# A Fourier stage whose first batch has a buffer of its own, filled in seven parts during the attention

## The chip, the cores and the metric

The kernel runs on one core of a Trainium2 chip. The metric is the device time of one execution in microseconds (us). The time before is the median of three runs.

## The reference

An attention, a Fourier mixing block with an MLP, and a gated block follow one another. `B`=4 batches, `H`=8 heads, `S`=576 positions, head size 64, width 512.

```python
scores = q @ k^T / sqrt(64) + bias
x = softmax(scores) @ v                       # (4, 576, 512)
mixed = real(fft(fft(x, axis=1), axis=2))
u = x + mixed
un = (u - mean(u)) / sqrt(var(u) + 1e-6)
y = u + relu(un @ w_ch1) @ w_ch2              # 512 -> 2048 -> 512
h = relu(y @ w_in); a, v = halves(h)
out = (a * (w_spatial @ norm(v) + b_spatial)) @ w_out
```

## The kernel before

The kernel makes the bias (to about 142 us), runs the attention, then the Fourier stage, then the MLP and the gated block. Only the attention's last two thirds and the Fourier stage are touched here.

**Attention** (`attention_phase`). It goes in 72 double steps `d` (two halves of a head's queries) through a software pipeline: scores on PE (line 408), row maximum on DVE (421), exponential `P` on ScalarE (444), one or more steps later. `P` has to be transposed for the product with `v`. For the even steps below 68 ScalarE (455) and POOL (461) cast `P` to an f16 tile `hl`, each a part of it, and a DMA transpose on SP's queue (474) makes `pt`; for the odd ones and the last four PE transposes `P` itself (484) and ScalarE (486) and DVE (493) evict it. PE multiplies (510), DVE normalises (539, 548) into `x`, and SP stores `x` into DRAM, one tensor `xd[b]` for a batch (560, 563). POOL also prepares the next head's operands (385, 387, 390, 393), ScalarE casts them (382, 383, 392). At the end of step `d` a hook `after(n)` is called with n = d - 72; it is `first_folds`.

**Fourier stage** (`Folds`, `fft_phase`). Real input makes it enough to work on sums and differences of a row and its mirror. `Folds.load(b)` reads `xd[b]` into a tile of six chunks of 128 rows: chunks 0 to 2 plain (rows 0 to 255, and 33 rows from 256; SP, lines 734, 735), chunks 3 to 5 the rows in reversed order, gathered by row number from POOL (line 737; 127, 128 and 32 rows), with single rows set to zero (732, 733). `Folds.steps` makes with DVE sums `T0` and differences `T1` of the two halves (748), the same along the width (`X0`, `X1`, 760), and the folds `F00` to `F11` (765). The names in the rows are `lowb` and `dif` for `T0` and `T1`, `uv`, `F`. On PE `stage1` makes four products for a batch, `pe`, `me`, `po`, `mo` (line 860), into one of two PSUM banks `y`, which ScalarE evicts (864). `corner(b)` copies one column of the tile to another (867, `raw<-raw 128x6`), `gather` makes `near` (871), which PE transposes into `xs` (878); `second` makes `D` (888), evicted as `d` (895), and DVE adds both (898, 906). Batch 0's load is made at n=-5, at the end of the attention, batch 1's at n=2, batch 2's at n=5, and some of batch 0's folds at n=3, 4, 5; batch 3's load is in the plan. Batch 0's tile is `raw`; those of batches 1 to 3 and the sums `T0` lie in `lowb`.

**What sets the order.** In the attention the order is the program's. In the Fourier stage a planner (`Plan.run`) sorts all operations, those of the first MLP weights (`w0` to `w3`) and of the layer norm among them: it takes each time the operation whose start, by given durations, less a bonus from the table `RANK` is least; `READY` gives the time from which a batch's tile counts as there. Each engine then works in its order, apart from what the compilation may move ahead where an operation depends on nothing between. A tile of MLP weights is loaded by SP (1676, `w<-in_w_ch`), squared on ScalarE (1015, `wsq<-w`) and split with DVE's help (1022 to 1028, 1684). The first MLP matmul is line 1339.

```python
    if d == nd:
        e1.close()
    after(d - nd)
```

Of the kernel before, what the change touches and what calls it, by code (L numbers as in the profile page):

```python
# [9 lines left out]
F32 = mybir.dt.float32  # L10
# [8 lines left out]
B, H, S, D = 4, 8, 576, 64  # L19
# [41 lines left out]
def pool(tc, **kw):  # L61

    return tc.tile_pool(reuse_waits="tile", **kw)
# [281 lines left out]
def attention_phase(tc, nc, io, vs, bias, biasl, raw, xd, ident, after, es, right):  # L345
# [206 lines left out]
    def store(d):  # L552
# [8 lines left out]
        for a in range(2):  # L561
            f = 128 * p + (64 * a if ahead(n) else 64 - 64 * a)
            nc.sync.dma_start(out=xd[b][512:S, f : f + 64], in_=x[64 * a : 64 * a + 64, 4, 0:64])

    yield [lambda n=n, nm=nm: load(n, nm) for n in range(2) for nm in "kqv"]
    yield from prep(0)
    yield True
# [13 lines left out]
    for d in range(nd + L5 + 2):  # L581
# [43 lines left out]
        if us and n + 2 < len(pairs):  # L625
            for nm in {0: "k", 1: "q", 2: "v"}.get(c - 5 * (c >= 5), ""):
                load(n + 2, nm)
# [7 lines left out]
def phases(tc, nc, io, vs, low, raw, xd, ident, tables, after, right):  # L635

    n = 2 * H * S
    bias = [x[:, 0:n].rearrange("p (t h s) -> p t h s", t=2, h=H) for x in low]
    biasl = low[1][:, n : n + NP * S].rearrange("p (h s) -> p h s", h=NP)
    with ExitStack() as es:  # L640
        att = attention_phase(tc, nc, io, vs, bias, biasl, raw, xd, ident, after, es, right)
        ready = False
        loads = next(att)

        def early(n):
            nonlocal ready
            if n >= Q_LOAD and loads:
                loads.pop(0)()
            if n >= T_LOAD:
                next(tables, None)  # L650
            if n in Q_PREP:
                ready = ready or next(att)

        with ExitStack() as e:
            bias_phase(tc, nc, io, vs, bias, biasl, early, e)
        while not ready:
            ready = next(att)
        for _ in att:
            pass
# [4 lines left out]
W_SCALE = 2.0**-112  # L664
TP = 290
T2 = 289
F_LOAD = -5
X_LOAD = 2, 5
FOLDS = {3: 3, 4: 3, 5: 2}
YB = 2  # L670
AFTER = (0,)
PRINT = False
RANK = {
# [4 lines left out]
}  # L678
READY = 0.0, 3.0, 8.0, 14.0


def tables(tc, nc, io, es):

    cp = es.enter_context(pool(tc, name="dft", bufs=1, side="right"))


    tt = cp.tile([128, 2, 3, TP], F32, name="tt")

    fs = cp.tile([128, 7, 128], F32, name="fs")
    ident = cp.tile([128, 128], F32, name="ident")  # L690
    rows = cp.tile([128, 3], I32, name="rows")

    def load():
        nc.gpsimd.dma_start(out=tt, in_=io["c_t"])
        yield
        for k in (slice(0, 4), slice(4, 7)):
            nc.sync.dma_start(out=fs[:, k], in_=io["c_f"][:, k])
            yield
        nc.sync.dma_start(out=ident, in_=io["c_ident"])
        nc.sync.dma_start(out=rows, in_=io["c_rows"])  # L700
        yield

    return (tt, fs, ident, rows), load()


class Folds:
# [19 lines left out]
        for F in self.two:  # L726
            self.nc.gpsimd.memset(F[1][:, :, 0:1], 0.0)

    def load(self, b):
        nc, x, d = self.nc, self.xs[b], self.xd[b]  # L730
        f = slice(1, DM + 1)
        nc.gpsimd.memset(x[32:33, 5, f], 0.0)
        nc.gpsimd.memset(x[0:1, 3, f], 0.0)
        nc.sync.dma_start(out=x[:, 0:2, f], in_=d[0:256].rearrange("(k p) d -> p k d", p=128))
        nc.sync.dma_start(out=x[0:33, 2, f], in_=d[256:T2])
        for k, r in ((3, slice(1, 128)), (4, slice(0, 128)), (5, slice(0, 32))):
            nc.gpsimd.indirect_dma_start(
                x[r, k, f], None, d[:, :],
                bass.IndirectOffsetOnAxis(ap=self.rows[0 : r.stop - r.start, k - 3 : k - 2], axis=0),
            )  # L740

    def steps(self, b):

        nc, x, F = self.nc, self.xs[b], self.two[b % 2]
        op = ALU.add, ALU.subtract

        def total(z):
            nc.vector.tensor_tensor(
                out=self.sums[z][:, :, 1 : DM + 1], in0=x[:, 0:3, 1 : DM + 1], in1=x[:, 3:6, 1 : DM + 1], op=op[z]
            )  # L750

        def mix(z):
            w = self.sums[z]

            def two(start, step):
                return bass.AP(
                    tensor=w.tensor, offset=w.offset + start, ap=[list(w.ap[0]), [DM + 2, 3], [step, 2], [-1, 129]]
                )

            nc.vector.tensor_tensor(out=self.uv[z], in0=two(256, 129), in1=two(513, -385), op=op[z])  # L760

        def fold(z, y):
            u, v = self.uv[z][:, :, 0], self.uv[z][:, :, 1, ::-1]
            o, r = (((0, slice(0, 129)), (129, slice(0, 128))), ((1, slice(1, 128)), (128, slice(1, 129))))[z][y]
            nc.vector.tensor_tensor(
                out=F[z][:, :, o : o + r.stop - r.start], in0=u[:, :, r], in1=v[:, :, r], op=op[y]
            )

        for z in range(2):
            yield f"T{z}", 1.75, lambda z=z: total(z)  # L770
            yield f"X{z}", 0.96, lambda z=z: mix(z)
            for y in range(2):
                yield f"F{z}{y}", 0.55, lambda z=z, y=y: fold(z, y)


def first_folds(folds):

    todo = []

    def after(n):  # L780
        if n == F_LOAD:
            folds.load(0)
        if n == 0:
            folds.open()
            todo.extend(folds.steps(0))
        if n in X_LOAD:
            folds.load(1 + X_LOAD.index(n))
        for _ in range(FOLDS.get(n, 0)):
            todo.pop(0)[2]()

    return after
# [45 lines left out]
def fft_phase(tc, nc, folds, tabs, ut, bank, extra, es):  # L837
# [28 lines left out]
    def corner(b):  # L866
        nc.scalar.activation(out=xs[b][:, :, 0:1], in_=xs[b][:, :, 256:257], func=AF.Copy)
# [45 lines left out]
    for b in range(B):  # L913
# [3 lines left out]
        if b:  # L917
            last = (b - 1, "F11") if b > 1 else None
            for nm, us, go in folds.steps(b):
                add_op(  # L920
                    (b, nm), f"fold{b}", [("DVE", us)], go, after=([last] if last else []) + (["load"] if b == B - 1 else []),
                    take=[f] if nm == "F00" else [], start=READY[b],
                )
                last = b, nm
        for nm, us, need in (("pe", 1.5, "F00"), ("me", 1.5, "F01"), ("po", 3.0, "F10"), ("mo", 1.5, "F11")):
# [7 lines left out]
            )  # L933
        add_op((b, "c"), "c", [("ACT", 0.2)], lambda b=b: corner(b), after=[(b, "T0")] if b else [], start=READY[b])
        for e in range(2):
# [819 lines left out]
def build(tc, io, out):  # L1755
    nc = tc.nc
    with ExitStack() as ctx:
        const = ctx.enter_context(tc.tile_pool(name="const", bufs=1))
        vs = const.tile([128, 1], F32, name="vs")
        low = const.tile([128, 16 * S], F32, name="lowa")  # L1760
        right = ctx.enter_context(ExitStack())
        tabs, load = tables(tc, nc, io, right)
        rp = right.enter_context(pool(tc, name="raw", bufs=1, side="right"))
        more = rp.tile([128, 20 * S], F32, name="lowb")
        raw = rp.tile([128, RAW], F32, name="raw")
        dp = ctx.enter_context(tc.tile_pool(name="dram", bufs=1, space=bass.MemoryType.DRAM))
        xd = [dp.tile([S, DM], F32, name=f"xd{b}") for b in range(B)]
        n, o = Folds.SIZE, 3 * Folds.SIZE
        folds = Folds(
            tc, nc, io, xd,  # L1770
            [raw[:, 0:n]] + [more[:, n * b : n * b + n] for b in range(B - 1)],
            more[:, o : o + Folds.SUM],
            tabs[3],
            right,
        )
        with ExitStack() as e1:
            e1.enter_context(tc.manual_schedule())
            phases(tc, nc, io, vs, (low, more), raw, xd, tabs[2], load, first_folds(folds), right)
        tail(tc, nc, io, folds, tabs, low, right, out, ctx)
# [138 lines left out]
```

## Time and profile before

| what | value |
|---|---|
| median of 3 runs | 1109.82 us (1108.58 to 1112.47) |
| profiled execution, time | 1107.36 us |
| its span | 1105.6 us |
| mean granted clock | 0.974 of full |
| PE busy | 1029.0 us (93%) |
| DVE, ACT, POOL busy | 686.4, 546.1, 311.4 us |
| PE `y`, `D` (lines 860, 888) in the chain of waits | 4%, 2% |

The profile shows one execution. Its page lists busy times, the span in 40 slices (among them the granted clock), the chain of waits that ended last, and groups of instructions; the rows below come from the finer views of the trace. A row of a timeline shows start, duration, engine, line, operation, output and input tiles, shapes, the count of equal instructions drawn together, and in brackets the idle time before it and what ended that. PE records two per f32 matmul.

### The profile page before, as it was taken

Reading aid. Unit: us, or ns where it says so; the run is one execution under the profiler, and the core shown is the slowest. Engines: PE = TensorE matmul, PEld = TensorE weight load, DVE = VectorE, ACT = ScalarE, POOL = GpSimd, SP = SyncE. Lnnn points to the kernel's source line nnn. Section 1 sums busy time; section 2 is a strip of 40 time slices with the busy share of each in tenths; the row PEclk is TensorE's granted clock in tenths of the full one; section 3 lists DMA queues with packets and bytes.
Section 4 is the critical chain, followed back from the end, with each engine's and each line's share of the span. In section 5 each row is a group of like instructions: output and inputs, shape, how many; then the busy total and the mean of one; then the engine's idle time right before and its main releaser. Section 6 shows DMA issues by size and latency. Waiting matters only on the chain.

```text
span 1105.6 us, 25371 instructions
## 1 busy us (share of the span) xinstructions
PE 1029.0 (93%) x10547; PEld 923.6 (84%) x10547; DVE 686.4 (62%) x1780; ACT 546.1 (49%) x1034; POOL 311.4 (28%) x271
## 2 busy tenths in 40 slices
PE   6999888888888689989999999999999999999998
PEld 4778777777787545689999999999999989998997
DVE  5998887878888457687894342334693275262612
ACT  3888797988898224553541121211353244333322
POOL 2777786868787230000000000000002030110000
PEclk8999899999999869999999999999999999999999
DMA  5542087878787630134540000000242000101011
GB/s 170 180 137 71 15 177 162 181 166 177 169 169 148 107 110 9 35 100 149 154 134 1 1 1 1 1 1 1 78 153 55 1 1 1 39 1 48 1 39 48
DMA packets 119615, 88.25 MB, mean 80 GB/s; under 512 B 89860, under 2 KB 100360, under 8 KB 119500
## 3 DMA queue, kind: packets, MB, share of 16 engines
q1 hardware_dynamic: 112024, 77.47, 28.1%
q10 hardware_dynamic: 2724, 5.90, 1.7%
q0 software_dynamic: 4752, 3.27, 1.1%
q8 instruction: 82, 1.34, 0.5%
q14 instruction: 33, 0.27, 0.1%
HBM read 57.10 MB, written 9.44 MB: 60 GB/s over the span
## 4 chain that ended last, share of the span: by engine, by line
PE 69%; DVE 11%; POOL 7%; DMA 6%; issue 4%; ACT 3%; SPq 0%; ACTq 0%; POOLq 0%; DVEq 0%
PE h L1339 18%; PE acc L1375 18%; PE psp L1511 5%; PE pu L1486 4%; PE po L1533 4%; PE y L860 4%; POOL hl L461 3%; PE pv L1434 3%; DMA pt<-hl 3%; PE sc L408 3%; PE po L510 2%; PE bps L267 2%; PE D L888 2%; PE turn L484 2%; PE pre L247 1%
## 5 line engine op out<-in xcount | busy, mean ns | idle before, releaser
L1343 ACT ACTIVATE gh<-h 128x256 fp32r<-128x256 f32 x144 | 54.9, 382 | 244.0 <-PE h L1339 240.1
L1344 DVE SCALAR_TENSOR_TENSOR gl<-h,gh 128x256 fp32r<-128x256 f32 x144 | 60.6, 422 | 170.5 <-ACT gh L1343 169.9
L1339 PE MATMUL h<-uh,wh 128*128 128x256 f32 x576 | 161.6, 281 | 2.7 <-DVE gl L1344 2.5
L1375 PE MATMUL acc<-gh,wh 128*128 128x256 f32 x576 | 163.2, 283 | 0.0
L1375 PE MATMUL acc<-gh,wl 128*128 128x256 f32 x576 | 161.2, 280 | 1.4 <-DVE wl L1047 1.4
L1339 PE MATMUL h<-uh,wl 128*128 128x256 f32 x576 | 161.0, 280 | 1.1 <-DVE wl L1047 1.1
L1375 PE MATMUL acc<-gl,wh 128*128 128x256 f32 x576 | 161.0, 279 | 0.0
L1339 PE MATMUL h<-ul,wh 128*128 128x256 f32 x576 | 160.8, 279 | 0.0
L1131 POOL MEMSET w<- 64x288 f32 x2 | 0.7, 338 | 421.2 <-DVE wsq L1028 421.2
L1339 PEld LDWEIGHTS h<-uh,wh 128*128 128x128 f32 x576 | 109.0, 189 | 3.5 <-DVE gl L1344 2.9
L1375 PEld LDWEIGHTS acc<-gh,wl 128*128 128x128 f32 x576 | 108.5, 188 | 1.7 <-DVE wl L1047 1.6
L1339 PEld LDWEIGHTS h<-uh,wl 128*128 128x128 f32 x576 | 108.5, 188 | 1.3 <-DVE wl L1047 1.3
L1375 PEld LDWEIGHTS acc<-gl,wh 128*128 128x128 f32 x576 | 109.0, 189 | 0.3
L1375 PEld LDWEIGHTS acc<-gh,wh 128*128 128x128 f32 x576 | 108.9, 189 | 0.4
L1339 PEld LDWEIGHTS h<-ul,wh 128*128 128x128 f32 x576 | 108.8, 189 | 0.0
L444 ACT ACTIVATE P<-s,mm 128x576 f32<-128x576 f32 x144 | 103.4, 766 | 4.6 <-DVE mm L436 3.7
L510 PE MATMUL po<-vp,pt 128*128 128x65 f16 (+3 forms) x2324 | 84.6, 196 | 12.6 <-DMA pt<-hl 9.9
L510 PEld LDWEIGHTS <-pt 128*128 128x128 f16 (+1 forms) x2324 | 81.0, 102 | 16.3 <-DMA pt<-hl 10.6
L461 POOL TENSOR_TENSOR hl<-P,hl 128x1024 f16<-128x1024 f32 x68 | 86.1, 1288 | 17.2 <-ACT hl L455 10.2
L484 PE MATMUL turn<-ident,P 128*128 128x128 f32 x380 | 58.9, 287 | 28.2 <-DVE pt L493 27.7
L484 PEld LDWEIGHTS turn<-ident,P 128*128 128x128 f32 x380 | 41.8, 144 | 40.7 <-PE sc L408 15.5
L250 ACT ACTIVATE mask<-pre 128x576 f16<-128x576 f32 x96 | 60.7, 651 | 24.2 <-PE pre L247 23.0
(247 smaller groups left out, 2612.4 us busy)
## 6 DMA issues: line engine op xcount, KB each, us to landing
w<-in_w_ch SPq DMA_DIRECT2D x32, 512.0 KB, 3.5
vld<-in_v ACTq DMA_DIRECT2D x16, 320.0 KB, 2.9
raw<-in_q SPq DMA_DIRECT2D x16, 320.0 KB, 5.8
raw<-in_v SPq DMA_DIRECT2D x16, 320.0 KB, 3.5
raw<-in_k SPq DMA_DIRECT2D x16, 288.0 KB, 6.0
xd<-x SPq DMA_DIRECT2D x16, 256.0 KB, 5.4
w<-in_w_in SPq DMA_DIRECT2D x8, 512.0 KB, 3.4
out<-o SPq DMA_DIRECT2D x16, 256.0 KB, 2.0
```

Of the source, the lines that this page charges most:

```text
L250: nc.scalar.activation(out=m.rearrange("p (x e) -> p x e", x=2), in_=p[:, :, 0:288], func=AF.Sigmoid, scale=1e30)
L444: nc.scalar.activation(out=P[:, x, 0:S], in_=s, func=AF.Exp, bias=mm[:, 1, x : x + 1], scale=1.0)
L461: nc.gpsimd.tensor_tensor(out=hl[:, :, o : o + c], in0=P[:, :, j : j + c], in1=hl[:, :, j : j + c], op=ALU.subtract)
L484: nc.tensor.transpose(t[:, 128 * k : 128 * k + 128], P[:, 128 * k : 128 * k + 128], ident)
L510: nc.tensor.matmul(out=po[c, t % 4, 0:w], lhsT=pt[:, x, c], rhs=vp[:, j, hh, f : f + w], start=(i == 0), stop=(i == len(seq) - 1),)
L860: nc.tensor.matmul(out=y[0:m, 0:TP], lhsT=st, rhs=mv, start=(n == 0), stop=(n == len(seq) - 1))
L1339: nc.tensor.matmul(out=h, lhsT=st[:, q], rhs=mv[:, k], start=(n == 0), stop=(n == 11))
L1343: nc.scalar.activation(out=gh, in_=h, func=AF.Relu)
L1344: nc.vector.scalar_tensor_tensor(out=gl, in0=h, scalar=0.0, in1=gh.bitcast(F32), op0=ALU.max, op1=ALU.subtract)
L1375: nc.tensor.matmul(out=acc[x, d // 2][:, d % 2], lhsT=st[:, q], rhs=mv, start=(e == 0 and d % 2 == 0 and n == 0), stop=(e == NF - 1 and d ...
L1486: nc.tensor.matmul(out=p[:, 0:CH], lhsT=st[:, q], rhs=mv[:, kk, e], start=(n == 0), stop=(n == 11))
L1511: nc.tensor.matmul(out=p[:, 0:CH], lhsT=st, rhs=mv, start=(n == 0), stop=(n == len(seq) - 1))
```

## The change

Batch 0 gets a tile of its own, `x0`, in SBUF; batch 1 takes `raw`, batches 2 and 3 the tile `lowb`. Batch 0's load no longer has to wait until `raw` and `lowb` are free of the attention. It is cut into seven parts (the zeros, three plain loads, three gathers), one at the end of each of the steps n=-36 to -30, that is d=36 to 42. Batch 1's load moves from n=2 to n=-2 and batch 2's from n=5 to n=2; batch 3's stays in the plan. Batch 0's folds are spread two by two over n=2 to 5. Each plain load of 256 rows becomes two of 128. `RANK` and `READY` have other numbers, which gives another order in the Fourier stage.

```diff
-F_LOAD = -5
-X_LOAD = 2, 5
-FOLDS = {3: 3, 4: 3, 5: 2}
+F_LOAD = -36
+X_LOAD = -2, 2
+FOLDS = {2: 2, 3: 2, 4: 2, 5: 2}
...
-    "y": 0.5, "me": 0.2, "po": -0.2, "mo": 0.8, "c": 31.6, "g": 0.1, "x1": 0.1, "d": 0.6, "+": 0.5, "r": 2.1,
+    "y": 0.4, "me": 0.3, "po": -0.2, "mo": 1.4, "c": 17.3, "g": -0.3, "x1": 0.7, "d": 0.4, "+": 0.5, "r": 3.6,
...
-    "-": 0.5, "fold1": 0.4, "fold2": 0.5, "load": 48.8, "fold3": -0.4, "w0": -0.2, "w1": 0.1, "w2": 0.8,
+    "-": 0.8, "fold1": 0.5, "fold2": 0.3, "load": 48.5, "fold3": 10.4, "w0": 1.3, "w1": -0.1, "w2": 1.0,
...
-READY = 0.0, 3.0, 8.0, 14.0
+READY = 0.0, 0.0, 3.0, 10.0
...
-    def load(self, b):
+    def loads(self, b):
...
-        nc.sync.dma_start(out=x[:, 0:2, f], in_=d[0:256].rearrange("(k p) d -> p k d", p=128))
-        nc.sync.dma_start(out=x[0:33, 2, f], in_=d[256:T2])
-        for k, r in ((3, slice(1, 128)), (4, slice(0, 128)), (5, slice(0, 32))):
+        def plain(k, r):
+            nc.sync.dma_start(out=x[0:r, k, f], in_=d[128 * k : 128 * k + r])
+
+        def turned(k, r):
             nc.gpsimd.indirect_dma_start(
                 x[r, k, f], None, d[:, :],
                 bass.IndirectOffsetOnAxis(ap=self.rows[0 : r.stop - r.start, k - 3 : k - 2], axis=0),
             )
+
+        yield zeros
+        for k, r in (0, 128), (1, 128), (2, 33):
+            yield lambda k=k, r=r: plain(k, r)
+        for k, r in (3, slice(1, 128)), (4, slice(0, 128)), (5, slice(0, 32)):
+            yield lambda k=k, r=r: turned(k, r)
...
-    todo = []
+    todo, loads = [], folds.loads(0)
 
     def after(n):
-        if n == F_LOAD:
-            folds.load(0)
+        if F_LOAD <= n < 0:
+            next(loads, int)()
...
+        x0 = rp.tile([128, Folds.SIZE], F32, name="x0")
...
-            [raw[:, 0:n]] + [more[:, n * b : n * b + n] for b in range(B - 1)],
+            [x0, raw[:, 0:n]] + [more[:, n * b : n * b + n] for b in range(B - 2)],
```

In the changed kernel the lines behind the edit have other numbers: 734 and 735 become 741, 737 becomes 744, 748 is 766, 860 is 878, 864 is 882, 867 is 885, 871 is 889, 888 is 906, 1015 is 1033, 1676 is 1694, 1684 is 1702.

How the order on the engines moves is seen at three places. The first is ScalarE in the middle of the attention, about 260 us in the trace of before: exponentials `P`, casts `kh`, `qh`, `hl` and evictions `pt`. Before:

```order
L382 ACTIVATE kh<-raw 128x576
L383 ACTIVATE qh<-raw 128x640
L444 ACTIVATE P_3270<-s,mm 128x576 x2
L486 ACTIVATE pt<-turn 128x640
L455 ACTIVATE hl<-P_3269 128x2x576
L444 ACTIVATE P_3271<-s,mm 128x576 x2
L486 ACTIVATE pt<-turn 128x640
```

and with the change (`x_72` is batch 0's tile, line 885 its corner copy):

```order
L382 ACTIVATE kh<-raw 128x576
L383 ACTIVATE qh<-raw 128x640
L444 ACTIVATE P_3271<-s,mm 128x576 x2
L486 ACTIVATE pt<-turn 128x640
L455 ACTIVATE hl<-P_3270 128x2x576
L444 ACTIVATE P_3272<-s,mm 128x576 x2
L885 ACTIVATE x_72<-x_72 128x6
L486 ACTIVATE pt<-turn 128x640
```

Batch 0's corner copy, which stood behind the attention as `raw<-raw`, now stands between the exponentials of d=42 and an eviction.

The second place is POOL in the same stretch, with the change; the rows `x_72<-xd_75,rows` are the three gathers of batch 0, the others were there before in the same order:

```order
L461 TENSOR_TENSOR hl<-P_3270,hl 128x2x64
L744 DMA x_72<-xd_75,rows 127x512
L461 TENSOR_TENSOR hl<-P_3272,hl 128x2x512
L461 TENSOR_TENSOR hl<-P_3272,hl 128x2x64
L385 TENSOR_TENSOR kl<-raw,kh 128x576
L744 DMA x_72<-xd_75,rows 128x512
L387 TENSOR_TENSOR ql<-raw,qh 128x640
L390 TENSOR_SCALAR raw<-raw,vs 128x640
L744 DMA x_72<-xd_75,rows 32x512
L461 TENSOR_TENSOR hl<-P_3270,hl 128x2x512
```

The gathers stand between the casts of `hl` and the preparation of the next head; the first follows the cast that starts at 254.66 us in the trace of before, the last comes ahead of the one at 265.94.

The third place is ScalarE at the start of the Fourier stage: evictions `y`, `near`, corner copies and the first MLP weights. Before:

```order
L486 ACTIVATE pt<-turn 128x640 x8
L867 ACTIVATE raw<-raw 128x6
L871 ACTIVATE near_8274<-raw 128x6x128 x2
L864 ACTIVATE y<-y 128x290
L871 ACTIVATE near_8275<-raw 128x6x128
L867 ACTIVATE lowb<-lowb 128x6
L864 ACTIVATE y<-y 128x290
L871 ACTIVATE near_8275<-raw 128x6x128
L871 ACTIVATE near_8274<-lowb 128x6x128 x2
L864 ACTIVATE y<-y 128x290
L1015 ACTIVATE wsq<-w_8600 128x512
```

and with the change:

```order
L486 ACTIVATE pt<-turn 128x640 x8
L885 ACTIVATE raw<-raw 128x6
L882 ACTIVATE y<-y 128x290
L1033 ACTIVATE wsq<-w_8601 128x512
L882 ACTIVATE y<-y 128x290
L889 ACTIVATE near_8285<-x_72 128x6x128
L1702 ACTIVATE wh<-wsq 128x512
L882 ACTIVATE y<-y 128x290 x2
```

The squaring `wsq` stood behind three evictions of `y` and stands now behind one; `near` comes later than it did.

## Rows read from the trace of the kernel before

**Rows 1.** PE's timeline, 330 to 480 us: start, us, engine, line, instruction, count.
```profile
366.80 0.94 PE L510 MATMUL po<-vp,pt 128*128 128x65 f16 x14 [9.17 <-DMA pt<-hl]
...
383.39 3.76 PE L860 MATMUL y<-tt,F 128*128 128x290 f32 x12 [0.18 <-PE po L510]
...
392.38 1.76 PE L878 MATMUL xs<-ident,near 128*128 128x128 f32 x6 [4.14 <-DVE x L539]
...
407.92 4.23 PE L888 MATMUL D<-y,fs 128*128 128x290 f32 x8
...
469.90 0.39 PE L1339 MATMUL h<-uh,wh 128*128 128x256 f32 x1
```
**Rows 2.** Busy time by stretch, then granted clock, DMA share, GB/s.
```profile
core 0: us, PE busy (x) PEld busy (x) DVE busy (x) ACT busy (x) POOL busy (x), PEclk, DMA share, GB/s
250.00:290.00 40.00, 36.46 (x625) 33.21 (x625) 34.87 (x103) 36.51 (x52) 30.48 (x22) 1.00 0.88 186
...
368.00:372.00 4.00, 3.75 (x50) 3.31 (x49) 2.27 (x5) 1.41 (x2) 3.51 (x3) 0.54 0.04 1
...
396.00:400.00 4.00, 4.00 (x8) 1.03 (x7) 1.41 (x3) 0.00 (x0) 0.00 (x0) 0.50 0.06 25
```
**Rows 3.** ScalarE's timeline, 258 to 425 us.
```profile
264.93 1.43 ACT L444 ACTIVATE P<-s,mm 128x576 f32<-128x576 f32 x2
...
347.54 1.16 ACT L455 ACTIVATE hl<-P 128x1152 f16<-128x1152 f32 x1
...
409.39 0.67 ACT L1015 ACTIVATE wsq<-w 128x512 f32<-128x512 f32 x1 [7.93 <-DMA w<-in_w_ch]
```
**Rows 4.** POOL's timeline, 235 to 425 us.
```profile
254.66 2.53 POOL L461 TENSOR_TENSOR hl<-P,hl 128x1024 f16<-128x1024 f32 x2
258.71 2.53 POOL L461 TENSOR_TENSOR hl<-P,hl 128x1024 f16<-128x1024 f32 x2 [1.51 <-PE sc L408]
...
265.94 2.53 POOL L461 TENSOR_TENSOR hl<-P,hl 128x1024 f16<-128x1024 f32 x2
...
345.68 0.52 POOL L732 MEMSET raw<- 1x512 f32 x1
...
346.96 2.66 POOL L737 DMA_INDIRECT raw<-xd,rows  x1 [0.20 <-issue]
...
352.11 2.53 POOL L461 TENSOR_TENSOR hl<-P,hl 128x1024 f16<-128x1024 f32 x2
...
368.44 2.58 POOL L737 DMA_INDIRECT lowb<-xd,rows  x1 [0.19 <-issue]
...
386.08 2.56 POOL L737 DMA_INDIRECT lowb<-xd,rows  x1 [11.51 <-issue]
```
**Rows 5.** SP's timeline, 290 to 425 us: DMA issues.
```profile
354.67 7.89 SPq L474 DMA_TRANSPOSE pt<-hl  x1
...
392.26 0.36 SPq L560 DMA_DIRECT2D xd<-x  x1
...
401.98 0.37 SPq L734 DMA_DIRECT2D lowb<-xd  x1
...
402.92 0.82 SPq L1676 DMA_DIRECT2D w<-in_w_ch  x2
```
**Rows 6.** The view of the tile `pt`, its DMA transposes.
```profile
DMA to landing us min/median/max: 4.6/5.3/6.4
```
**Rows 7.** DVE's timeline, 370 to 425 us.
```profile
387.40 1.76 DVE L748 TENSOR_TENSOR lowb<-lowb 128x1536 f32<-128x1536 f32 x1 [2.44 <-DMA lowb<-xd]
...
391.55 0.68 DVE L539 TENSOR_TENSOR x<-po,ri 128x512 f32<-128x512 f32 x1
...
402.66 1.76 DVE L748 TENSOR_TENSOR lowb<-lowb 128x1536 f32<-128x1536 f32 x1 [5.21 <-DMA lowb<-xd,rows]
```
**Rows 8.** The page's DMA issues: line, KB each, us to landing.
```profile
xd<-x SPq DMA_DIRECT2D x16, 256.0 KB, 5.4
```
**Rows 9.** The chain of waits, 340 to 500 us: start, us, what.
```profile
432.36 5.36 PE y L860 x18
437.72 2.18 PE xs L878 x12
```

More of the change, by code (lines that the diff above doesn't have):

```diff
@@ L727, in open, with zeros @@
             self.nc.gpsimd.memset(F[1][:, :, 0:1], 0.0)
-    def load(self, b):
+    def loads(self, b):
         nc, x, d = self.nc, self.xs[b], self.xd[b]
         f = slice(1, DM + 1)
-        nc.gpsimd.memset(x[32:33, 5, f], 0.0)
-        nc.gpsimd.memset(x[0:1, 3, f], 0.0)
-        nc.sync.dma_start(out=x[:, 0:2, f], in_=d[0:256].rearrange("(k p) d -> p k d", p=128))
-        nc.sync.dma_start(out=x[0:33, 2, f], in_=d[256:T2])
-        for k, r in ((3, slice(1, 128)), (4, slice(0, 128)), (5, slice(0, 32))):
+        def zeros():
+            r = slice(32, 33) if b else slice(0, 128)
+            nc.gpsimd.memset(x[r, 5, f], 0.0)
+            if b == 0:
+                nc.gpsimd.memset(x[r, 2, f], 0.0)
+            nc.gpsimd.memset(x[0:1, 3, f], 0.0)
+        def plain(k, r):
+            nc.sync.dma_start(out=x[0:r, k, f], in_=d[128 * k : 128 * k + r])
+        def turned(k, r):
             nc.gpsimd.indirect_dma_start(
@@ L740, in load @@
             )
+        yield zeros
[3 more added lines that the diff above has]
+            yield lambda k=k, r=r: turned(k, r)
+    def load(self, b):
+        for go in self.loads(b):
+            go()
     def steps(self, b):
@@ L1765, in build @@
         raw = rp.tile([128, RAW], F32, name="raw")
+        x0 = rp.tile([128, Folds.SIZE], F32, name="x0")
         dp = ctx.enter_context(tc.tile_pool(name="dram", bufs=1, space=bass.MemoryType.DRAM))
         xd = [dp.tile([S, DM], F32, name=f"xd{b}") for b in range(B)]
-        n, o = Folds.SIZE, 3 * Folds.SIZE
+        n, o = Folds.SIZE, 2 * Folds.SIZE
         folds = Folds(
             tc, nc, io, xd,
-            [raw[:, 0:n]] + [more[:, n * b : n * b + n] for b in range(B - 1)],
+            [x0, raw[:, 0:n]] + [more[:, n * b : n * b + n] for b in range(B - 2)],
             more[:, o : o + Folds.SUM],
```

4 rows, old and new, of the table RANK are left out of this document.

## The prediction

> **What bounds the kernel now.** I first read the page's busy times and its 40 slices: TensorE is the bound nearly everywhere, so only a stretch in which PE idles or runs at the low clock can be shortened. Then I read PE's timeline from 340 to 480 us, where the change acts. The reader is to see two idle times and one stretch at a low clock there [rows 1]: 9.17 us before 366.80 (ended by the landing of a transposed P tile), 4.14 us before 392.38 (ended by the last attention output on DVE), and matmuls that take twice as long until about 412 (the 8 of `D` there take 4.23 us). [...] The first MLP matmul starts at 469.90; everything behind it is untouched by the change, so the question is by how much that start moves.
>
> **The first idle time.** Batch 0's three gathers stand on POOL between two `hl` casts. ScalarE has written its half of `hl` at 347.54+1.16=348.70, but POOL is in the gathers and starts its half at 352.11, 3.41 us late [rows 3, 4]. The transpose behind it is issued at 354.67 [rows 5] and lands 12.1 us later (PE resumes at 366.80), where the tile view gives 4.6, 5.3 and 6.4 us as least, median and most [rows 6]. With the three gathers gone from this place the transpose is issued at 354.67-3.41=351.26 and lands between 356.6 and 357.7; PE wants it at 366.80-9.17=357.63. **-9.2 us**, at the worst -9.1. The clock of 0.54 at 368 to 372 goes too; of the 16.6 us of drain behind it (to 383.39) most is waiting between engines, so I take 0.6 us for it, bounds 0 and 1.7 (3.75 us of PE work at 0.54 instead of 1). The FFT's first matmul comes at 383.39-9.2-0.6=373.6, before anything is added.
>
> **The second idle time.** In the kernel before DVE waited 2.44 us, to 387.40, for batch 1's load [rows 7]. Its gather is now issued right behind the last casts but two memsets, at about 351.2+1.3=352.5 (345.68 to 346.96 is 1.3) instead of 368.44. A 127-row gather lands 16.6 us after its issue (386.08 to DVE's 402.66, [rows 4, 7]), or at the most the 19.8 us from 346.96 to PE's 366.80; so at 369 to 372.3. DVE wants it at 387.40-2.44-9.8=375.2. **The 2.44 us go**, and the last attention output, which followed at 391.55+0.68=392.23, ends at 392.23-9.8-2.44=380.0.
>
> **What is added in the attention: ScalarE.** The new buffer frees batch 0's corner copy (128x6) of everything but batch 0's load, and the order rows show it between two exponentials of the attention. It reads all of the tile, so it waits for all three gathers. ACT comes to it at 264.93+1.43=266.36 [rows 3]. POOL is free for the first gather at 254.66+2.53=257.19 [rows 4]; with 0.2 us of issue it goes at 257.4. By 16.6 us it lands at 274.0, by 19.8 at 277.2: ACT stands still for 7.6 to 10.8 us. The least is given by the third gather's issue: behind the first, POOL has 7.23 us of its own work (258.71 to 265.94) and the 5.15 us that three gathers held it at 346.96 to 352.11, so the third leaves at 257.2+7.23+5.15=269.6, and ACT loses 3.2 us even if it lands at once. Behind the waiting copy stand the exponentials, and on those PE's flips, POOL's casts and the transposes. ACT is busy 36.51 of 40 us here and PE 36.46 [rows 2]: neither has spare time to speak of, so PE loses nearly all of it. The gather rows are nearest, and the three gathers queue one behind the other, so I take 8.5 us of stall and half a microsecond won back by the idle 9%: **+8 us**, bounds 3 and 11. The seven parts' other costs: three plain DMAs on SP, each holding its queue for the 0.4 us of such an issue [rows 5], and three memsets of 0.52 us on POOL, which is busy 30.48 of 40 us: nothing; without that cover the memsets cost 1.6 us, which lies inside the bounds.
>
> **What is added at the FFT's start: a wait for the weights.** ScalarE's order now has the squaring of the first MLP weight tile (`wsq<-w`, line 1033) ahead of the second eviction of `y`. There are two `y` banks, so PE's fourth product `mo` stands behind that squaring. The weight's DMA is on SP behind batch 3's load, and that waits for the landing of the last attention store. In the kernel before: store issued 392.26, load released 401.98 (9.72 us), weight issued 402.92 (0.94), squaring 409.39 (6.47) [rows 3, 5]. It cost PE nothing then, since PE was working at the low clock through all of it. Now: store at 380.0. Its landing took 9.72 us against 5.4 in the median of its kind [rows 8], and was some 0.7 us before batch 2's gather landed (402.66). Batch 2's gather now goes one gather period (368.44 to 386.08, 17.6 us) behind 352.5, at 370.1, and lands at 386.7 at the soonest. So the store lands between 386.0 and 389.8; I take 388. Weight issued 388.9, squaring 395.4, its 0.67 us and a little less for the eviction: `mo` at **396.5**. PE has `pe`, `me` (3.8 us) from 373.6 to 377.4 and `po` (the same number of records) from about 380.5, since DVE makes the odd folds right behind the attention output, to 384.3. It idles 3.1 and then 12.2 us.
>
> [...]
>
> **The rest of the FFT.** Behind `mo` the work is that of 412.15 to 469.90 of the kernel before (57.75 us at full clock) and what had been done there before 412.15 and not yet here: 12 records of `y` at 5.36/18, 12 of `xs` (2.18), 8 of `D` (4.23 at the low clock, so 2.1) [rows 1, 9], 7.9 us: 65.7 in all. The clock will have fallen in the idle time, as it did twice: after 9.17 us idle it was low for some 4.9 us (the stretch from 368 to 372 has 0.54 on average, a loss of 2.5), after 4.14 us for 20 us, to 412.15 (a loss of 10). I take 6, between them. End: 396.5+65.7+6=468.2, against 469.9: **-1.7 us**, with bounds of -7.2 (store at 386, loss 2.5) and +4.1 (389.8, loss 10).
>
> **Sum.** -1.7+8=+6.3 us. The profiled execution took 1107.36 us (its span 1105.6, 1.8 around it), so 1113.7; the median of the three runs, 1109.82, is 2.46 above that execution, so the forecast is **1116 us**. Its own range, most of both bounds, is 1111 to 1122. About 0.3% (3.3 us) is what a measurement of this kernel can tell from no change.
>
> **Rivals.**
> (1) *The loads in the attention come nearly free.* If the 127-row gather were spread over the DMA engines, the copy on ACT would wait just for the third gather's issue, 3.2 us, of which the idle 9% of the next 40 us (3.5) wins part back: +0 to +3 us. Against it: while such a gather was alone in flight the DMA share was 0.06, one of 16 engines, at 25 GB/s [rows 2]. For it: transposes have 0.88 of all DMA time here, and a short stall may be taken by the three score buffers. With the FFT's -1.7 to -6 this is 1104 to 1111. Chance 0.2, of which 0.08 faster.
> [...]
> (2) *The weights don't bind* (the other side: faster). If the squaring's input is there when PE ends `po`, about 384, the `y` eviction passes and PE idles just the 3.1 us. Then the FFT's 86.5 us (383.39 to 469.90) lose the 4.14 us idle and 10 of low clock and keep 72.4; from 373.6, with 3.1 idle and at least 2.5 of low clock, that ends at 451.6: -18.3, and with +8 in the attention -10.3, 1099. It decides at a landing at 384; the store alone, at 380.0 plus its 5.4, denies it, unless the output comes earlier. Chance 0.12.
> (3) *The attention loses more.* The transposes issued while the gather is in flight land late, as the one at 354.67 did (12.1 instead of 5.3, 6.8 us more), and that comes after ACT's wait instead of under it: +11 to +15 in place of +8, 1119 to 1123, up to 1127 with the FFT's upper bound. Chance 0.1.
>
> **How the numbers follow.** Forecast 0.58 (0.06 of it within 0.3%), rivals 0.2, 0.12 and 0.1. The likeliest time is 1116. The range from 1103 to 1123 takes in the forecast and rival 1, and leaves out rival 2 and the tail of rival 3, some 0.15. Faster: 0.12+0.08=0.20. Within 0.3%: 0.12+0.06=0.18. Slower: 0.52+0.1=0.62.
>
> **What would show it.** In the changed kernel's profile: ACT idle 7 to 11 us before the 128x6 copy near 266, ended by the landing of a gather, and PE with a gap of the like behind it (no gap: rival 1); PE's gap of 9 us near 358 (plus the shift) gone, and the transpose landing in 4.6 to 6.4 us; DVE's second batch's first sum without a wait; the squaring on ACT waiting for `w<-in_w_ch` with PE idle over 10 us before `mo` (none: rival 2); granted clock 0.5 behind it. The MLP's first matmul then starts at 476. A start before 470 or behind 484 would make the forecast wrong.

## The result

The changed kernel takes 1120.85 us (median of 15 runs, 1115.54 to 1127.40), the kernel before 1115.84 us beside it (15 runs, 1108.58 to 1121.70). The ratio is 1.0056, 95% interval 1.0029 to 1.0083: slower by 6.2 us, 3.2 to 9.3. The forecast was +6.3 us and 1116, the range 1103 to 1123. (The three runs shown ahead, with 1109.82 as their median, were low ones for the kernel before.)

The two traces are cut at three events: the first product of `P` and `v`, the first FFT matmul, the first MLP matmul. In PE's timeline of the kernel before the first of them is

```profile
142.33 1.02 PE L510 MATMUL po<-vp,pt 128*128 128x65 f16 x28
```

and the other two stand in [rows 1]. PE's timeline of the changed kernel:

```profile
145.11 1.02 PE L510 MATMUL po<-vp,pt 128*128 128x65 f16 x28
...
269.31 1.71 PE L510 MATMUL po<-vp,pt 128*128 128x65 f16 x28 [2.43 <-DMA pt<-hl]
...
283.58 1.33 PE L484 MATMUL turn<-ident,P 128*128 128x128 f32 x5 [6.93 <-DVE pt L493]
...
391.96 3.76 PE L878 MATMUL y<-tt,F 128*128 128x290 f32 x12
398.76 5.26 PE L878 MATMUL y<-tt,F 128*128 128x290 f32 x12 [3.04 <-DVE F L783]
414.22 7.05 PE L878 MATMUL y<-tt,F 128*128 128x290 f32 x12 [10.20 <-ACT y L882]
...
484.98 0.39 PE L1357 MATMUL h<-uh,wh 128*128 128x256 f32 x1
```

The reader is to see that both idle times of [rows 1] are gone (nothing of 9 us ahead of the drain, no wait of 4 us for the last attention output) and that new ones stand in the list: 2.43 and 6.93 us in the middle of the attention, 3.04 us ahead of `po`, and 10.20 us ahead of `mo`, ended by the eviction of `y`. From the first product to the first FFT matmul it is 246.8 us instead of 241.1, from there to the MLP 93.0 instead of 86.5. What follows is the same (635.1 and 635.7 us).

The attention gained at its end and lost in its middle. To see both, take ScalarE's exponentials, of which every trace has 172 in the same order. In the changed kernel the 91st starts just ahead of batch 0's gathers and the 127th behind the stall. These two, in the kernel before and then with the change:

```profile
253.14 1.43 ACT L444 ACTIVATE P<-s,mm 128x576 f32<-128x576 f32 x2
...
300.35 1.43 ACT L444 ACTIVATE P<-s,mm 128x576 f32<-128x576 f32 x2
```
```profile
256.78 1.43 ACT L444 ACTIVATE P<-s,mm 128x576 f32<-128x576 f32 x2
...
317.98 1.43 ACT L444 ACTIVATE P<-s,mm 128x576 f32<-128x576 f32 x2
```

The middle (from the 91st to the 127th) takes 47.2 us before and 61.2 with the change, 14.0 more. The end (from the 127th to the first FFT matmul) takes 83.0 us before and 74.0 with the change, 9.0 less. The second traces (e11, e12) give 13.3 more and 10.6 less. PE's busy time and clock in the two middles (columns as in [rows 2]):

```profile
253.14:300.35 47.21, 41.54 (x717) 37.58 (x714) 39.81 (x117) 42.81 (x62) 37.65 (x28) 1.00 0.82 172
```
```profile
256.78:317.98 61.20, 45.71 (x695) 41.20 (x691) 39.20 (x114) 43.00 (x63) 42.31 (x31) 0.86 0.85 153
```

PE idles 5.7 us in the first and 15.5 in the second; the other 4.2 us are longer PE work, at a granted clock of 0.86 instead of 1.00. The second trace lacks some records of PE (695 of 717), so this split is rough.

ScalarE's timeline shows what holds the engine at the new ones, where [rows 3] had no gap at 266 and a squaring that nobody waited for:

```profile
268.57 1.43 ACT L444 ACTIVATE P<-s,mm 128x576 f32<-128x576 f32 x2
281.86 0.21 ACT L885 ACTIVATE x<-x 128x6 f32<-128x6 f32 x1 [11.87 <-DMA pt<-hl]
...
395.27 0.39 ACT L882 ACTIVATE y<-y 128x290 f32<-128x290 f32 x1
413.20 0.66 ACT L1033 ACTIVATE wsq<-w 128x512 f32<-128x512 f32 x1 [17.54 <-DMA w<-in_w_ch]
413.77 0.40 ACT L882 ACTIVATE y<-y 128x290 f32<-128x290 f32 x1
```

A copy of 0.21 us holds ACT for 11.87 us. The profile puts that down to a landing of `pt`, which the copy does not read. The copy does read what the gathers bring. POOL's timeline has the first and the third of them:

```profile
261.00 2.66 POOL L744 DMA_INDIRECT x<-xd,rows  x1 [0.19 <-DMA raw<-in_v]
...
272.32 0.92 POOL L744 DMA_INDIRECT x<-xd,rows  x1 [0.17 <-issue]
```

The third landed 9.4 us behind its issue, at 281.7, just ahead of the copy (the run with spread gathers, below, names the gather). The squaring holds the second eviction of `y`: ACT idles 17.54 us ahead of it.

The granted clock in the stretches of the first stall (columns as in [rows 2]):

```profile
268.00:276.00 8.00, 6.69 (x81) 6.17 (x83) 2.23 (x7) 2.00 (x3) 7.57 (x6) 0.57 1.17 43
276.00:284.00 8.00, 1.07 (x12) 0.84 (x11) 1.30 (x2) 2.14 (x5) 0.62 (x1) 0.69 1.18 221
284.00:292.00 8.00, 7.35 (x92) 6.56 (x90) 5.29 (x17) 6.24 (x10) 4.45 (x4) 0.67 0.60 140
```

The clock went down in the stall (0.57 to 0.69 of full in these 24 us, where the kernel before had 1.00 from 250 to 290): the forecast had no term for that. SP's timeline shows the weight's chain, to be held against [rows 5]:

```profile
398.18 0.38 SPq L560 DMA_DIRECT2D xd<-x  x1
...
407.06 1.23 SPq L741 DMA_DIRECT2D lowb<-xd  x3
408.40 7.77 SPq L1694 DMA_DIRECT2D w<-in_w_ch  x3
```

Store to load 8.9 us, weight 1.3 us behind it, squaring 4.8 us after that.

### The profile page after: what moved, and what is told of

It is laid out like the page before. It is cut to its first block, busy times and chain, and to the rows that moved or that the text cites. A ratio compares the mean times of both kernels' runs of the same rounds, so it can differ in the third digit from the quotient of the medians.

```text
span 1120.1 us, 25387 instructions
## 1 busy us (share of the span) xinstructions
PE 1034.0 (92%) x10547; PEld 928.6 (83%) x10547; DVE 689.0 (62%) x1780; ACT 547.2 (49%) x1034; POOL 313.2 (28%) x272
## 4 chain that ended last, share of the span: by engine, by line
PE 66%; DVE 11%; POOL 10%; issue 6%; DMA 4%; ACT 3%; SPq 0%; ACTq 0%; POOLq 0%; DVEq 0%
PE h L1357 18%; PE acc L1393 17%; PE psp L1529 5%; POOL hl L461 5%; PE pu L1504 4%; PE po L1551 4%; PE pv L1452 3%; PE y L878 3%; PE bps L267 2%; PE D L906 2%; PE pre L247 2%; PE xs L896 2%; PE po L510 1%; DVE bt L311 1%; DVE mask L235 1%
## 5 line engine op out<-in xcount | busy, mean ns | idle before, releaser
L510 PE MATMUL po<-vp,pt 128*128 128x65 f16 (+3 forms) x2324 | 87.0, 198 | 4.1 <-DMA pt<-hl 2.8
L510 PEld LDWEIGHTS <-pt 128*128 128x128 f16 (+1 forms) x2324 | 83.6, 103 | 7.8 <-DMA pt<-hl 3.5
L493 DVE TENSOR_TENSOR pt<-turn,pt 128x640 f16<-128x640 f32 x76 | 62.0, 821 | 21.0 <-ACT pt L486 21.0
```

The source lines that it names most:

```text
L493: nc.vector.tensor_tensor(out=pt[:, 5:10], in0=t, in1=pt[:, 0:5], op=ALU.subtract)
L510: nc.tensor.matmul(out=po[c, t % 4, 0:w], lhsT=pt[:, x, c], rhs=vp[:, j, hh, f : f + w], start=(i == 0), stop=(i == len(seq) - 1),)
```

## The experiments

Twelve runs. The timed ratios are against the kernel before, measured beside it on the same chip; the three events and the stages are from the traces. Middle and end are parts of the attention, as defined above.

| kernel | ratio (95%) | first P.v | first FFT | first MLP | attention | its middle | its end | FFT |
|---|---|---|---|---|---|---|---|---|
| before | 1 | 142.33 | 383.39 | 469.90 | 241.1 | 47.2 | 83.0 | 86.5 |
| before again (e11) | - | 147.51 | 389.36 | 475.43 | 241.9 | 46.7 | 84.5 | 86.1 |
| changed | 1.0056 (1.0029 to 1.0083) | 145.11 | 391.96 | 484.98 | 246.8 | 61.2 | 74.0 | 93.0 |
| changed again (e12) | - | 148.00 | 393.26 | 486.09 | 245.3 | 60.0 | 73.9 | 92.8 |
| e1 corner copy late | 1.0038 (1.0003 to 1.0073) | 142.96 | 383.90 | 476.16 | 240.9 | 57.3 | 72.9 | 92.3 |
| e2 weights first | 1.0001 (0.9970 to 1.0032) | 143.43 | 387.96 | 476.71 | 244.5 | 60.0 | 72.9 | 88.8 |
| e3 128-row gathers | 0.9900 (0.9843 to 0.9956) | 145.57 | 383.31 | 469.99 | 237.7 | 53.3 | 73.8 | 86.7 |
| e4 old tables | 0.9980 (0.9939 to 1.0022) | 145.18 | 389.06 | 472.87 | 243.9 | 59.4 | 72.8 | 83.8 |
| e5 before, 128-row gathers | 0.9824 (0.9768 to 0.9881) | 144.28 | 375.57 | 458.21 | 231.3 | 46.7 | 73.9 | 82.6 |
| e6 late copy and 128 rows | 0.9923 (0.9898 to 0.9947) | 144.03 | 378.96 | 465.21 | 234.9 | 49.9 | 72.3 | 86.2 |
| e7 e6 and old tables | 0.9872 (0.9837 to 0.9907) | 146.60 | 381.72 | 457.73 | 235.1 | 52.3 | 72.3 | 76.0 |
| e8 e6 and weights first | 0.9893 (0.9852 to 0.9934) | 144.80 | 379.62 | 464.31 | 234.8 | 51.7 | 72.3 | 84.7 |
| e9 e7, loads at the end | 0.9898 (0.9859 to 0.9936) | 143.26 | 380.11 | 463.80 | 236.9 | 47.1 | 79.0 | 83.7 |
| e10 e5 again | 0.9879 (0.9833 to 0.9926) | 143.49 | 378.54 | 461.14 | 235.1 | 46.7 | 77.6 | 82.6 |

**e1, the corner copy behind the attention.** The copy is issued at n=5 instead of from the plan.

```diff
+        if n == 5:
+            x = folds.xs[0]
+            folds.nc.scalar.activation(out=x[:, :, 0:1], in_=x[:, :, 256:257], func=AF.Copy)
...
     def corner(b):
+        if b == 0:
+            return
```

> Changed kernel, but batch 0's corner copy on ScalarE is issued behind the attention (at n=5), everything else as it is. Theory A (the copy waiting for the three gathers holds ACT, and ACT everything): the 11.87 us idle before it near 282 us goes, PE's 6.93 us gap near 283 and the low clock from 268 to 292 go; the first FFT matmul comes 10 to 15 us earlier than in the changed kernel, and the time falls by about 1%, to some 0.5% under the kernel before. Rival B (the loads themselves cost the time: the one-engine gather holds the DMA transposes, POOL loses 6 us to it): the gap on PE in that place stays at 5 us or more, ended by a landing of pt, and the time falls by less than 0.4%.

The attention fell from 246.8 and 245.3 to 240.9, so by 4 to 6 us and not by 10 to 15; the time by 0.2%. Its middle takes 57.3 us, where the four traces with the waiting copy (changed, e12, e2, e4) have 59.4 to 61.2 and the kernel before 47.2 and 46.7. PE's timeline keeps waits in that place:

```profile
268.81 1.71 PE L510 MATMUL po<-vp,pt 128*128 128x65 f16 x28 [4.79 <-DMA pt<-hl]
...
278.23 1.03 PE L510 MATMUL po<-vp,pt 128*128 128x65 f16 x28 [2.31 <-DMA pt<-hl]
```

Neither reading holds alone, but the rival is nearer: without the waiting copy some 10 of the 13 us lost in the middle remain, and the late transposes, which the copy's wait had covered, come to light when it goes.

**e2, the first weight tile ahead of batch 3's load on SP.**

```diff
-    "-": 0.8, "fold1": 0.5, "fold2": 0.3, "load": 48.5, "fold3": 10.4, "w0": 1.3, "w1": -0.1, "w2": 1.0,
+    "-": 0.8, "fold1": 0.5, "fold2": 0.3, "load": 1.0, "fold3": 10.4, "w0": 1.3, "w1": -0.1, "w2": 1.0,
```

> Changed kernel with the rank of batch 3's load at 1.0 instead of 48.5, so that SP issues the first weight tile ahead of that load; the orders on PE and ACT stay. Theory A (mo waits for the squaring, that for the weight's DMA, that for the store's landing): the weight is issued within 2 us of the last store instead of 10, PE's 10.2 us gap before mo shrinks to 2 to 5 us, the FFT ends 5 to 8 us earlier, the time falls by about 0.5%, to near the kernel before. Rival (the gap is paid anyway, since batch 3's load now comes later and PE waits for that): the gap before mo shrinks and one of the same size comes later in the FFT; time unchanged within 0.2%.

SP and PE:

```profile
394.18 0.38 SPq L560 DMA_DIRECT2D xd<-x  x1
...
395.86 0.52 SPq L1694 DMA_DIRECT2D w<-in_w_ch  x1
```
```profile
405.81 7.06 PE L878 MATMUL y<-tt,F 128*128 128x290 f32 x12 [4.15 <-ACT y L882]
```

The weight goes out 1.7 us behind the store, `mo` waits 4.15 us instead of 10.20 and 9.31, and the FFT is 4 us shorter (88.8 against 93.0 and 92.8), a little less than the 5 to 8 expected. Most of what the wait loses is gained in the stage, and no wait of that size comes later; the rival falls. The chain from the store over the weight to the eviction is shown.

**e3, 128-row gathers.** A row of zeros is added to each DRAM tensor, and the first gather takes it for its first partition; the memset of that partition goes. In this run the index table of that gather was off by one row in the other partitions; it moves the same bytes in the same pieces, and from e5 on the rows are the right ones.

```diff
-        for k, r in (3, slice(1, 128)), (4, slice(0, 128)), (5, slice(0, 32)):
+        for k, r in (3, slice(0, 128)), (4, slice(0, 128)), (5, slice(0, 32)):
...
-        xd = [dp.tile([S, DM], F32, name=f"xd{b}") for b in range(B)]
+        xd = [dp.tile([S + 1, DM], F32, name=f"xd{b}") for b in range(B)]
...
+        for d in self.xd:
+            self.nc.sync.dma_start(out=d[S : S + 1], in_=self.io["c_nul"])
```

> Changed kernel; each batch's gather of 127 rows is made one of 128 rows (the first takes a row of zeros that is added to the DRAM tensor), the memset of that row goes. Theory A (127 rows go over one DMA engine and hold what is in flight): the copy's wait on ACT shrinks from 11.9 to 3 to 6 us, transposes near it land in 4.6 to 6.4 us, the gathers of batches 1 to 3 land within 6 us of issue, store to load takes 5 to 6 us instead of 8.9, mo comes 4 to 6 us earlier after the first FFT matmul; time lower by 0.8 to 1.2%, under the kernel before. Rival (the gather's time is set by indirect addressing, not by the number of rows): gathers still land 16 us after issue, time unchanged.

The view of the gathers' line, first in the changed kernel, then here:

```profile
DMA to landing us min/median/max: 9.4/15.0/18.0
```
```profile
DMA to landing us min/median/max: 5.1/5.7/9.7
```

One row more, and the median from issue to landing falls from 15.0 to 5.7 us; the issue itself takes POOL 1.07 us instead of 2.66. ACT and PE:

```profile
275.83 0.21 ACT L890 ACTIVATE x<-x 128x6 f32<-128x6 f32 x1 [6.17 <-DMA x<-xd,rows]
```
```profile
399.91 7.05 PE L883 MATMUL y<-tt,F 128*128 128x290 f32 x12 [2.89 <-ACT y L887]
```

The copy's wait falls from 11.87 to 6.17 us, now with the gather as its releaser, `mo` waits 2.89 us instead of 10.20, and the kernel is 1% faster than the kernel before. From store to load it is 2.3 us on SP (389.54 to 391.79) instead of 8.9, less than the 5 to 6 expected. One part of the expectation failed: the transposes near the gathers were to land in 4.6 to 6.4 us. The view of `pt` and PE's timeline show that one still lands late and is waited for:

```profile
DMA to landing us min/median/max: 4.5/4.9/10.1
```
```profile
270.42 1.70 PE L510 MATMUL po<-vp,pt 128*128 128x65 f16 x28 [3.87 <-DMA pt<-hl]
```

The middle takes 53.3 us: some 7 of the 13 us come back. That the 127-row gather runs on one engine is read from its DMA share alone in flight, 0.06 or one of 16 [rows 2]. The 128-row ones were seen in e5: from 362 to 364 us, behind a gather issued at 361.53 and with the next store issued at 363.35, the share is 0.35 at 92 GB/s, that of 5.6 engines on average. In this sense they are called spread here.

**e4, the old tables on the changed loads.** `RANK` and `READY` of the kernel before, the rest of the changed kernel.

> Changed loads, but RANK and READY of the kernel before. It shows the loads' move alone. Theory A: ACT's wait in the attention stays (10 us or more); in the FFT the squaring stands behind three evictions, so the gap before mo goes and is at most 4 us, the FFT is 5 us or more shorter than in the changed kernel from its first matmul to the MLP's; time about 0.5% under the changed kernel, near the kernel before. Rival (the new tables fit the new load times better, and the old order waits elsewhere): FFT as long or longer than in the changed kernel, time the same or above.

The FFT takes 83.8 us, less than in either kernel, and no wait stands ahead of `mo`:

```profile
389.06 3.76 PE L878 MATMUL y<-tt,F 128*128 128x290 f32 x12
...
397.09 13.92 PE L878 MATMUL y<-tt,F 128*128 128x290 f32 x24
```

So the loads' move alone is worth nothing that can be measured in the time (0.9980): what it loses in the middle it gains at the end and in the FFT. The new tables cost the rest. Of the 9 us between 93.0 and 83.8 the weight's place on SP is 4 (e2); the other 5 go with the order as a whole and were not taken apart.

**e5, the kernel before with 128-row gathers.** The same edit as e3 on the kernel before, with the right rows.

```diff
-        for k, r in ((3, slice(1, 128)), (4, slice(0, 128)), (5, slice(0, 32))):
+        for k, r in ((3, slice(0, 128)), (4, slice(0, 128)), (5, slice(0, 32))):
...
-    p[:, 0] += 1
```

> Kernel before with the 127-row gathers made 128-row ones (first row: a row of zeros added to the DRAM tensor); nothing else. My reading (the transpose at 354.67 landed late because the 127-row gather holds one DMA engine): that transpose lands in 4.6 to 6.5 us instead of 12.1, PE's gap of 9.17 us falls to 3 us or less (the 3.4 us by which POOL is late stay), the second gap of 4.14 goes since batch 1's load lands sooner; first FFT matmul 6 to 9 us earlier, time lower by 0.5 to 0.9%. Rival (the transpose was late because it shares the engines with the stores and loads, whoever gathers): gap of 8 us or more stays, time within 0.2%.

SP's and PE's timelines at the end of the attention:

```profile
354.99 3.43 SPq L474 DMA_TRANSPOSE pt<-hl  x1
```
```profile
360.48 0.60 PE L510 MATMUL po<-vp,pt 128*128 128x65 f16 x14 [0.36 <-DMA pt<-hl]
...
375.57 3.76 PE L865 MATMUL y<-tt,F 128*128 128x290 f32 x12 [0.18 <-PE po L510]
```

PE resumes 5.5 us behind the issue of that transpose, where it took 12.1 us in the kernel before (the trace has no landing of its own for this one); the wait of 9.17 us [rows 1] is 0.36, though the gathers stand between POOL's casts as before. The attention is 9.8 us shorter, the FFT 3.9, the time 1.8% lower, more than the 0.5 to 0.9% expected. So the first idle time that the change was to remove was not made by the gathers' place on POOL, but by the one gather's 127 rows.

**e6, both (128 rows and late copy) on the changed kernel.**

> Changed kernel with both the 128-row gathers and batch 0's corner copy behind the attention. In the earlier runs the time from the first P.V matmul to the first FFT matmul was 246.9 us in the changed kernel, 240.9 with the copy late and 237.7 with the gathers spread. Theory A' (the copy's wait and the one-engine gather are all that the attention lost): 231 to 234 us with both. Rival (POOL's and SP's extra work costs by itself): 236 or more. FFT stage as with the spread gathers, 86 to 87 us; time 1.0 to 1.5% under the kernel before.

234.9 us lies between the two, and the time is 0.8% lower, not 1.0 to 1.5. The middle decides for the rival: it takes 49.9 us here, 52.3 in e7 and 51.7 in e8, where five traces without loads in that place (before, e5, e9, e10, e11) have 46.7 to 47.2. So with the copy late and the gathers spread the loads there still cost 3 to 5 us. PE waits for a transposed tile in all three; e7's timeline has the longest wait:

```profile
271.32 1.71 PE L510 MATMUL po<-vp,pt 128*128 128x65 f16 x28 [4.04 <-DMA pt<-hl]
```

**e7, e6 with the tables of the kernel before.**

> As the run with both (128-row gathers, late copy), and RANK and READY of the kernel before. With the old tables the FFT took 83.8 us instead of 93.0 on one-engine gathers. If the wait for the weights was all that the new tables cost, the FFT comes to 79 to 83 us here; attention as in the run with both. Time 1.3 to 2% under the kernel before. If the new tables suit fast gathers better, the FFT is 86 us or longer.

76.0 us, below the forecast's 79: the clock did not fall. Just ahead of batch 0's last product PE idled about as long in e5 and in e7; PE's timeline of e5, then of e7:

```profile
382.03 1.13 PE L883 MATMUL xs<-ident,near 128*128 128x128 f32 x6 [1.61 <-DVE x L539]
383.09 13.03 PE L865 MATMUL y<-tt,F 128*128 128x290 f32 x24
```
```profile
388.06 1.13 PE L906 MATMUL xs<-ident,near 128*128 128x128 f32 x6 [1.48 <-DVE x L539]
389.11 7.49 PE L886 MATMUL y<-tt,F 128*128 128x290 f32 x24
```

The same 24 records take 13.03 us in e5, whose granted clock is 0.72 from 384 to 415 us, and 7.49 in e7, the rate of the 12 that take 3.76 us in the kernel before [rows 1], at a clock of 1.00.

**e8, e6 with the first weight tile ahead of batch 3's load.**

> As the run with both (128-row gathers, late copy), the new tables, but the first weight tile issued ahead of batch 3's load. With fast gathers the store's landing is short, so the weight comes only some 2 us sooner: FFT 84 to 87 us, 0 to 3 us shorter than in the run with both; if mo's wait is no longer set by the weight, no difference.

84.7 against 86.2: 1.5 us, as expected with a short store.

**e9 and e10, e7 with batch 0's loads at the attention's end in its own buffer, and e5 once more.**

```diff
-X_LOAD = -2, 2
+X_LOAD = 0, 2
...
-        if F_LOAD <= n < 0:
+        if n == -12 or -5 <= n <= 0:
```

> 128-row gathers, late copy, tables of the kernel before, as in the run with old tables, but batch 0's loads are not made in the middle of the attention: the zeros at n=-12, the plain loads at n=-5 to -3, the gathers at n=-2 to 0, behind the last casts; batch 1's load at n=0, batch 2's at n=2. If the loads in the middle cost 3.6 us by taking POOL and SP (234.9 and 235.1 us against 231.3 with the loads at the end), the attention takes 231 to 232 us here and the FFT 80 to 82: time 0.3% under the run with old tables, 1.5 to 2% under the kernel before. If batch 0's data come too late now, DVE's first sum waits and the FFT starts later.

> The kernel before with 128-row gathers once more, beside the run with the own buffer at the end on the same chip. Attention 231 us and FFT 86 us from the first trace; if the low clock at the FFT's start is not in every execution, the FFT varies between 80 and 86 us and this kernel is within 0.5% of that one.

e9's attention takes 236.9 us, and my expectation of 231 to 232 fell. But its middle takes 47.1 us, as in the kernel before: moving the loads out of the middle gained the 3 to 5 us that e6 to e8 had left there. They were lost again at the end, which takes 79.0 us where e6 to e8 have 72.3. In e10, the same kernel as e5, the end takes 77.6 us where e5 had 73.9. PE's timeline of e10:

```profile
358.68 0.61 PE L510 MATMUL po<-vp,pt 128*128 128x65 f16 x14 [0.46 <-DMA pt<-hl]
...
378.54 3.76 PE L865 MATMUL y<-tt,F 128*128 128x290 f32 x12 [0.18 <-PE po L510]
```

The wait for the transposed tile is gone as in e5, but from there to the first FFT matmul it is 19.9 us instead of 15.1; why, these traces do not settle. So loads with spread gathers cost 3 to 5 us in the middle (e6 to e8), and at the end between 1.6 (e5) and 6.7 (e9) over the 72.3 us; the totals, 231.3 to 236.9 us in these six traces, do not tell the two places apart. e10's FFT is 82.6 like e5's (not 86, as the expectation has it). The intervals of e5, e7, e9 and e10 overlap; no version with the own buffer is shown to beat the kernel before with 128-row gathers, which is 1.2 to 1.8% faster than the kernel before.

**e11 and e12, both kernels for a second trace.**

> The kernel before, unchanged, for a second trace: its first trace (1107.36 us) lies below its median of 1114 to 1116 us over many runs. If the two stages account for the result, the attention again takes 241 us and the FFT 86, and the rest of the difference lies in what the change does not touch (the bias phase, the MLP).

> The changed kernel, unchanged, for a second trace: attention 245 to 249 us, FFT 91 to 95; ACT's wait before the corner copy 10 us or more, PE's gap before mo 8 us or more. If these differ by over 3 us, a single trace is no measure of the terms.

Both stages come out within 1.6 us of the first traces. What moves between executions is the bias phase: the first product starts at 142.33 and 147.51 in the kernel before, at 145.11 and 148.00 in the changed one.

## Why the prediction was right, and where it was not

The direction and the mechanisms were right. The first idle time came out as forecast, the FFT's term 1.5 us too large, and ScalarE's term in the attention, outside its bounds, 5.6 us too small. That the timed difference (6.2 us) meets the forecast's 6.3 is in part luck: in the traces the stages add up to 11.2 us on average.

**The first idle time, -9.8 with the clock.** It held. The end of the attention takes 83.0 and 84.5 us in the kernel before, 74.0 and 73.9 in the changed one: 9.8 less in the mean. I had the gathers' place on POOL (3.4 us) as part of the cause; in e5 and e10 the gathers stand in that place and PE's wait is 0.36 and 0.46 us, so the one-engine gather made it. The landing times of [rows 6] on which I leaned are those of 8 of the 34 transposes; the trace has none for the others.

**The second idle time.** It went as said. The last attention output was to end 6.4 us behind the first FFT matmul; the store was issued 6.2 behind it (398.18 less 391.96).

**ScalarE in the attention, +8, bounds 3 and 11.** This step was too small: the middle takes 61.2 and 60.0 us instead of 47.2 and 46.7, so 13.6 more. First, the stall was 11.87 and 11.43 us where I took 8.5 and had 10.8 as the most: I let the copy wait 16.6 to 19.8 us from the first gather's issue, but the last of the three landed 20.7 us behind it (261.00 to 281.7). Second, the low clock of 0.57 to 0.69 in the stall had no term. Third, transposes that land late beside the loads had been left to rival 3 (e1's waits of 4.79 and 2.31 us; up to 11.0 us to landing there). Its +11 to +15 is what came. The experiments take the 13 us apart, from a mean of 60.2 us in the four traces with one-engine gathers and waiting copy: spread gathers bring the middle to 53.3 (e3), the late copy as well to 51.3 (mean of e6 to e8), the loads moved to the end to 47.1 (e9). These are 6.9, 2.0 and 4.2 us; with the one-engine gather left in, the late copy is worth 2.9 (e1).

**The wait for the weights.** From the first FFT matmul to `mo` I had 22.9 us; the traces have 22.3 and 23.0. Idle ahead of `po` 3.1 forecast, 3.04 measured; ahead of `mo` 12.2 forecast, 10.20 and 9.31 measured. The FFT stage was to grow by 8.1 us (468.2 less 373.6, against 86.5); it grew by 6.5 and 6.7. The step was right in mechanism, and e2 shows it.

**Sum.** In the traces the two stages give +12.3 and +10.2 us, 4 to 6 us over the forecast's +6.3: 5.6 us from ScalarE's term and 0.8 from ahead of the 91st exponential, less 1.5 from the FFT's. The timed difference, 3.2 to 9.3 us, agrees with the forecast better than the traces do. Part of that is chance in which executions were profiled: the kernel before's traces (1107.36 and 1114.01 us) lie below its medians of 1111 to 1116 on average, the changed kernel's (1121.90 and 1124.61) above its 1120.85. The rest stays open. The time itself, 1120.85, lies in the range but 4.9 us over the 1116, mainly because the kernel before takes 1115.84 and not the 1109.82 from which I counted.

**The signs.** One went against the forecast as it is worded: the MLP's first matmul starts at 484.98 and 486.09, behind the limit of 484. Part of that lies ahead of the first product of `P` and `v`, in the bias phase, which the change does not touch. Counted from that product the MLP starts after 339.9 and 338.1 us, before it was 327.6 and 327.9; the limit is then 341.7 and the forecast 333.9. DVE's first sum of batch 1 has no wait, as said.

**Rivals.** Rival 1's condition, a gather spread over the engines, was made in e3: the copy waits 6.2 us, not 3.2, and the middle loses 6.3 us (53.3 against 47.0) and not 0 to 3. The DMA share of 0.88 that it gives to the transposes is that of all transfers in the stretch, the loads of `raw` and the stores among them. Rival 2's condition came true with the old tables (e4): FFT 83.8, and with fast gathers 76.0 (e7), on both sides of the 78.0 (451.6 less 373.6) worked out there. Rival 3's upper end is added up too low: 1123 with the FFT's upper bound, 5.8 us above its middle, is 1129 and not 1127.

## What to carry to other kernels

Look at the landing times of every gather and at the number of its partitions: one row more (127 to 128) brought the median landing from 15.0 to 5.7 us (e3) and the time of the kernel before down by 1.8 and 1.2% (e5, e10), more than all moving about of that load (0.2%, e4). Loads moved into a busy stretch cost there too (3 to 5 us here, even with spread gathers), so a gain at one end has to be set against it. When an operation is freed of a wait by a new buffer, look in the order of its engine for where it goes now: a 0.2 us copy that runs ahead into a busy stretch holds everything behind it until its own input is there (11.87 and 11.43 us here). And an operation that waits for a DMA does not belong between two evictions of a two-bank PSUM tile (`mo` waited 10.20 and 9.31 us for that here).

## What the runs showed that was not expected

With batch 0's loads in the middle of the attention a transpose there lands late, whether the gather beside it runs on one engine or is spread: at most 8.4, 9.3 and 11.0 us in the changed kernel's two traces and in e1, and 10.1, 7.6, 10.0 and 9.5 in e3, e6, e7 and e8, against 6.4 and 6.6 at most in the two traces of the kernel before (each trace has landings for 6 to 8 of its 34 transposes). Which of the loads delays it was not taken apart. Of the clock in the kernel before: when PE ran again after 9.17 us of idle it was back within some 5 us (0.54 from 368 to 372 us, 1.00 from 372 to 376), after 4.14 us only after 20 (0.50 from 392.4 to 412). By the time of the 24 records, after nearly equal idle times of 1.61 and 1.48 us it fell in one trace (e5, 13.03 us) and stayed in the other (e7, 7.49 us), with what ran before them alike but not the same (in e4 it fell behind 1.48 us, as the 13.92 us for the same 24 records show); what decides that, these runs do not show. And one kernel's attention varies by 3.8 us between executions (e5, e10), another's bias phase by 5.2 (before, e11), so that differences of a few us between single traces need a second one.
